# Adding 1e-9 to the row sums with a tensor-tensor operation, and converting the early weights one stage at a time

## The chip, the core and the metric

The kernel runs on one core of a Trainium2 chip. Five engines work side by side, each through its own queue in order: PE (TensorE, the matrix engine), DVE (VectorE), ACT (ScalarE), POOL (GpSimd) and SP (SyncE, which here issues the DMAs). They wait for each other by semaphores. The metric is the device time of one execution in microseconds (us).

## What is computed

Attention with a decay, and two feed-forward layers behind it, in 32-bit numbers:

```python
# attention: B, H, S, D = 4, 8, 576, 64
scores = matmul(q, k^T) / sqrt(D) + cum[:, None] - cum[None, :]   # cum = cumsum(log(clip(f)))
attn = exp(causal(scores) - rowmax)
attn = attn / (sum(attn) + 1e-9)
x = matmul(attn, v)                       # 2304 tokens x 512
# first layer: d_ff = 2048
x = softplus(x @ w_in) @ w_out
# second layer: d_ff = 1536
out = (sigmoid(x @ w_gate) * (x @ w_val)) @ w2_out
```

The weights arrive as 64-bit floating point numbers and are converted on the chip. Every 32-bit operand of a matmul is split into a high part in the matmul's own type and a low remainder, so that a product is three matmuls.

## The kernel before

**Attention.** The heads are taken two at a time: 16 pairs (p = 0 to 15). Of one pair, PE makes the score tiles (`scores`, L209 and L220, tile s), DVE adds the mask and finds the row extremes (`minimum`, L227, out to P and m), ACT takes exponentials and row sums (`exp`, L232), PE transposes P (`transposes`, L250, tile t, seven groups 0 to 6 that share two buffers), ACT takes the high part out of t (`evac_h`, L268, into PTah or PTbh), DVE the low part (`evac_l`, L272, into PTal or PTbl), which also frees the buffer of t, and PE multiplies with V (`pv`, L322, tile x). `rinv` (L275 to L280) adds 1e-9 to the nine columns of row sums of a pair (L278, a tile of 128x9) and takes the reciprocal (L279); PE transposes it (L284, tile rt, which takes one of the two t buffers), ACT copies it out (L289), and it goes through DRAM to be spread over rows. POOL splits q, k and v for coming pairs (L160 for the high parts Xh, Yh and V; L168 for the low parts Xl, Yl and V) and multiplies a finished pair with the reciprocal (L340, xs).

**The order of the work.** It is written out by hand: `WHEN` gives each step of a pair a time in units, a pair begins every `PERIOD` = 9 units, and the steps of all pairs, with a list `others` of (time, function), are sorted by time and issued in that order. `START` and `END` replace `WHEN` for the first and the last pair. So a number in these tables sets where an instruction stands in its engine's queue, and nothing else.

**Early weights.** Six blocks of the first layer's weights (wi0, wo0, wi1, wo1, wi2, wo2, each 128x512) are converted during the attention. `Weights` keeps seven stages for a block: LOAD (L463, a DMA of 512 KB issued by SP into one of four raw buffers), SCALE (ACT, L471), SHIFT, LOW, SIGN (DVE, L485, L487, L489: bit operations on 128x512 words that put the 64-bit number together; SHIFT has one input tile, LOW and SIGN have two, raw and w, all in SBUF), HI (ACT, L476) and LO (POOL, L479). `op(s)` does one stage for the next block that waits for it, and does nothing if none does; `tick` goes through all stages once. `TICKS` holds eight times of such ticks, and `LATE_TICKS` those behind the attention. Since SHIFT, LOW and SIGN are issued one behind the other in a tick, DVE does all three for one block in a row. I call that a burst; the eight ticks make six bursts.

**Behind the attention** come the two layers, where PE has matmuls to do nearly all the time.

Of the kernel before, what the change touches and what calls it, by code (L numbers as in the profile page):

```python
# [9 lines left out]
F32 = mybir.dt.float32  # L10
# [3 lines left out]
ALU = mybir.AluOpType  # L14
# [7 lines left out]
class Attention:  # L22
# [13 lines left out]
    def pools(self, pool, io_pool):  # L36
        self.vp = pool("at_v", 2)
        self.pp = pool("at_p", 2)
        self.sm = pool("at_small", 3)
        self.xp = pool("at_x", 2)  # L40
        self.io = io_pool("at_io", 2)
# [40 lines left out]
    def constants(self):  # L82

        nc, c, S = self.nc, self.c, self.S
        self.qrs = [c.tile([128, 640], F32, name=f"qr{i}") for i in range(2)]
        for q in self.qrs:
            nc.gpsimd.memset(q[0:64, 576:640], 0.0)
            nc.gpsimd.memset(q[64:128, 512:576], 0.0)
        self.nbs = [c.tile([128, S], F32R, name=f"nb{i}") for i in range(2)]
        nc.gpsimd.memset(self.nbs[0][64:128].bitcast(F32), 0.0)  # L90

        self.one = c.tile([128, 256], F32R, name="one")
        o = self.one[:].bitcast(F32)
        nc.gpsimd.memset(o, 0.0)
        for r, t in ((0, 128), (64, 192)):
            nc.gpsimd.memset(o[r:r + 2, 0:128], 1.0)
            nc.gpsimd.memset(o[r:r + 2, t:t + 64], 1.0)

        self.mask = c.tile([128, 512], F32, name="mask")
        nc.gpsimd.memset(self.mask, 0.0)  # L100
        nc.gpsimd.affine_select(self.mask, self.mask, pattern=[[-1, 512]], compare_op=ALU.is_ge,
                                fill=-8e9, base=384, channel_multiplier=1)
        self.mask4 = c.tile([128, S], F32, name="mask4")

    def constants2(self):
        nc, c, S = self.nc, self.c, self.S
        nc.gpsimd.memset(self.mask4, 0.0)
        for i in range(2):
            M = self.mask4[64 * i:64 * i + 64]
            nc.gpsimd.affine_select(M, M, pattern=[[-1, S]], compare_op=ALU.is_ge, fill=-8e9, base=512,  # L110
                                    channel_multiplier=1)
        nc.gpsimd.memset(self.nbs[1][:].bitcast(F32), 0.0)
        ident = c.tile([128, 128], F32, name="ident")
        nc.gpsimd.memset(ident, 0.0)
        nc.gpsimd.affine_select(ident, ident, pattern=[[-1, 128]], compare_op=ALU.not_equal,
                                fill=1.0, base=0, channel_multiplier=1)
        self.ident = ident

        self.vr = [c.tile([128, 5, 128], F32, name=f"vr{i}") for i in range(self.NVR)]
        for t in self.vr:  # L120
            nc.gpsimd.memset(t[64:128, 4], 0.0)
        self.pta = [[c.tile([128, 1152], F32R, name=f"PTa{w}{i}") for w in "hl"] for i in range(2)]
        self.ptb = [c.tile([128, 2368], F32R, name=f"PTb{w}") for w in "hl"]
        for t in self.ptb:
            for o, n in ((768, 128), (1792, 128), (2304, 64)):
                nc.gpsimd.memset(t[:, o:o + n].bitcast(F32), 0.0)
# [148 lines left out]
    def rinv(self, R, p):  # L275
        nc = self.nc
        r = self.sm.tile([128, 9], F32, tag="r", name=f"r{p}")
        nc.vector.tensor_scalar(r, R["sum"], 1e-9, None, op0=ALU.add)  # L278
        nc.vector.reciprocal(r, r)  # L279
        R["r"] = r  # L280

# [423 lines left out]
class Moe2:  # L705
# [53 lines left out]
    STEPS = 10  # L759
# [176 lines left out]

TICKS = [-79.5479, -7.81, 1.0296, 20.4876, 29.246, 38.239, 47.3352, 87.6118]
LATE_TICKS = [-7.39, 35.9211, 42.3787, 45.7979, 60.2136, 64.0078, 68.4722, 70.489, 70.7365, 71.6392, 73.755, 76.4625, 83.1312, 92.4907, 95.2063, 99.2562, 116.366, 144.939, 153.168, 159.446, 198.508]  # L940
X_STEPS = [-50.0345, -24.888, -24.7421, -11.1038, -4.6076, -2.1888, 2.7229, 20.2706]
UNITS = [58.5061, 83.1125]
# [3 lines left out]
def kernel(ctx: ExitStack, tc, q, k, v, f, w_in, w_out, w_gate, w_val, w2_out, out):  # L946
    nc = tc.nc
# [17 lines left out]
    W = Weights(nc, stage, 4)  # L965
# [10 lines left out]
    with ExitStack() as actx:  # L976
        ioctx = ExitStack()
        right = pools(actx, side="right")
        at = Attention(nc, q, k, v, f, xT, right, ps, dr)
        at.pools(right, pools(ioctx, side="right"))  # L980
        at.begin()
        end = at.PERIOD * at.NP
        m1 = []

        def open_pools():
            ioctx.close()
            chain = pool("chain", 1, **later)
            wb = pool("wb", 1, **later)
            W.add_slots(wb, tags("b", 2 * MORE))
            W.limit = EARLY + MORE  # L990
            m1.extend([chain, Moe1(nc, FC1, x1, yT, W, chain, ps)])

        others = [(t, W.tick) for t in TICKS] + [(end + t, W.tick) for t in LATE_TICKS]
        others += [(end + t, lambda k=k: x1.step(0, k)) for k, t in enumerate(X_STEPS)]
        others += [(end - .5, open_pools)]
        others += [(end + t, lambda u=u: m1[1].unit(u, 0)) for u, t in enumerate(UNITS)]
        at.run(others)
# [131 lines left out]
```

## Time and profile before

| | before |
|---|---|
| median of 3 runs | 1063.03 us (1062.92 to 1065.11) |
| profiled execution, its time and its span | 1063.44 us, span 1061.7 us |
| PE busy | 1027.5 us (97%) |
| DVE busy | 678.9 us (64%) |
| ACT busy | 455.2 us (43%) |
| POOL busy | 155.4 us (15%), all in the first 240 us |

The page's picture in 40 slices of 26.5 us shows PE at 4, 9, 9 and 8 tenths in the first four and at 9 (90% or more) from then on, DVE at 9 in slices 2 to 7, and POOL busy in the first nine slices alone. So the attention takes about the first 230 us, and what PE lacks is mostly in the first 100. An average over the whole span tells nothing here; the rows below are of stretches of the attention. A stretch is named by its start, and most are cut at the L278 of one pair and that of the next.

### The profile page before, as it was taken

The page shows a single profiled execution, that of the slowest core. Times are in us where ns is not written, and L with a number is a line of the kernel's source. Part 1 is how long each engine was busy: PE and PEld are TensorE (multiplying, and loading weights), DVE is VectorE, ACT ScalarE, POOL GpSimd, SP SyncE. Part 2 cuts the span into 40 slices and gives each one's busy share as a digit, 9 for nine tenths or more (in the row PEclk, how much of TensorE's full clock was granted, in tenths as well). Part 3 has the DMA queues.
Part 4 walks back from the last instruction along what each step waited for, and adds up shares of the span by engine and source line. Part 5 has one row for each costly group of instructions (what it writes and reads, how often), then busy time and mean ns, then how long its engine had stood idle before and what let it go on. Part 6 is the DMA issues. An engine that isn't in the chain of part 4 may idle for free.

```text
span 1061.7 us, 17894 instructions
## 1 busy us (share of the span) xinstructions
PE 1027.5 (97%) x6376; PEld 924.9 (87%) x6376; DVE 678.9 (64%) x1453; ACT 455.2 (43%) x989; POOL 155.4 (15%) x158
## 2 busy tenths in 40 slices
PE   4989999989999999999999999999999999999998
PEld 3767888878889999999999998999999999899997
DVE  5899999978955755745755556655655656555421
ACT  4678888866644434344343442222222222221121
POOL 7656777440000000000000000000000000000000
PEclk9999999999999999999999999999999999999999
DMA  6354454445534565564563599997887886686481
GB/s 167 94 151 128 130 145 125 130 138 183 188 128 172 197 233 178 192 236 170 193 225 126 201 358 362 341 314 248 279 262 231 288 261 230 228 296 215 141 274 63
DMA packets 129492, 218.23 MB, mean 206 GB/s; under 512 B 16174, under 2 KB 46526, under 8 KB 129404
## 3 DMA queue, kind: packets, MB, share of 16 engines
q1 hardware_dynamic: 126364, 212.08, 61.0%
q10 hardware_dynamic: 3040, 5.01, 1.4%
q8 instruction: 50, 0.82, 0.3%
q14 instruction: 38, 0.31, 0.1%
HBM read 171.21 MB, written 45.83 MB: 204 GB/s over the span
## 4 chain that ended last, share of the span: by engine, by line
PE 88%; DVE 7%; ACT 2%; issue 1%; DMA 1%; POOL 0%; ACTq 0%; SPq 0%; DVEq 0%; POOLq 0%
PE h L540 7%; PE h L541 7%; PE h L539 7%; PE s L220 5%; PE h_S L541 4%; PE h_S L539 4%; PE h_S L540 4%; PE x L322 4%; PE t L250 4%; PE h_A L539 3%; PE h_A L541 3%; PE h_A L540 3%; PE zX L900 3%; PE zX L901 2%; PE zX L902 2%; PE oY L540 2%
## 5 line engine op out<-in xcount | busy, mean ns | idle before, releaser
L541 PE MATMUL h<-xh,wi_l 128*128 128x448 f32 (+1 forms) x320 | 118.4, 370 | 0.0
L540 PE MATMUL h<-xl,wi_h 128*128 128x448 f32 (+1 forms) x320 | 118.4, 370 | 0.0
L539 PE MATMUL h<-xh,wi_h 128*128 128x448 f32 (+1 forms) x320 | 118.4, 370 | 0.0
L581 DVE TENSOR_TENSOR gl<-L,gh 128x448 fp32r<-128x448 f32 (+1 forms) x80 | 50.9, 637 | 99.4 <-ACT gh L580 88.5
L876 ACT CAST gh<-bl 128x512 fp32r<-128x512 f32 (+1 forms) x60 | 34.6, 579 | 168.6 <-DVE bl L847 141.5
L569 ACT ACTIVATE L<-h 128x448 f32<-128x448 f32 (+1 forms) x80 | 44.2, 552 | 142.3 <-PE h L541 131.1
L232 ACT ACTIVATE P<-P,m 128x128 f32<-128x128 f32 (+3 forms) x144 | 83.4, 583 | 13.1 <-DVE m L227 13.1
L540 PE MATMUL h_S<-x,ring 128*128 128x256 f32 x288 | 81.5, 283 | 0.0
L227 DVE CUSTOM_DVE_ANT_0 P<-s,mask 128x256 f32<-128x256 f32 (+3 forms) x144 | 70.7, 517 | 15.5 <-PE s L220 10.5
L539 PE MATMUL h_S<-x,ring 128*128 128x256 f32 x264 | 74.7, 283 | 0.0
L541 PE MATMUL h_S<-x,ring 128*128 128x256 f32 x264 | 74.7, 283 | 0.0
L250 PE MATMUL t<-ident,P 128*128 128x128 f32 x400 | 62.6, 293 | 7.0 <-DVE PTbl L272 4.0
L541 PEld LDWEIGHTS h<-xh,wi_l 128*128 128x128 f32 x320 | 60.1, 188 | 6.3
L539 PEld LDWEIGHTS h<-xh,wi_h 128*128 128x128 f32 x320 | 60.1, 188 | 6.3
L540 PEld LDWEIGHTS h<-xl,wi_h 128*128 128x128 f32 x320 | 60.1, 188 | 6.3
L250 PEld LDWEIGHTS t<-ident,P 128*128 128x128 f32 x400 | 47.0, 148 | 19.7 <-DVE PTbl L272 5.7
L845 ACT ACTIVATE bh<-bh 128x1024 f32<-128x1024 f32 x24 | 25.4, 1060 | 89.4 <-DVE bh L843 89.4
L681 DVE TENSOR_TENSOR l<-fw,sh 128x512 fp32r<-128x512 f32 x60 | 40.7, 686 | 35.8 <-ACT sh L680 35.7
L540 PEld LDWEIGHTS h_S<-x,ring 128*128 128x128 f32 x288 | 55.3, 192 | 0.0
L833 DVE TENSOR_TENSOR L<-h_S,L 128x256 f32<-128x256 f32 x48 | 20.3, 423 | 53.3 <-PE h_S L541 49.9
L540 PE MATMUL h_A<-x,ring 128*128 128x256 f32 x192 | 54.3, 283 | 0.0
L877 DVE TENSOR_TENSOR gl<-bl,gh 128x512 fp32r<-128x512 f32 (+1 forms) x60 | 38.0, 635 | 24.9 <-ACT gh L876 24.9
(233 smaller groups left out, 3079.5 us busy)
## 6 DMA issues: line engine op xcount, KB each, us to landing
ring<-sd_g SPq DMA_DIRECT2D x192, 256.0 KB
ring<-sd_v SPq DMA_DIRECT2D x192, 256.0 KB
raw_wi<-in_moe_w_in_dram SPq DMA_DIRECT2D x16, 512.0 KB
raw_wo<-in_moe_w_out_dram SPq DMA_DIRECT2D x16, 512.0 KB
fraw<-in_moe_w_gate_dram SPq DMA_DIRECT2D x12, 512.0 KB
fraw<-in_moe_w_out_dram SPq DMA_DIRECT2D x12, 512.0 KB
sd_g<-sh SPq DMA_DIRECT2D x24, 256.0 KB
sd_g<-l SPq DMA_DIRECT2D x24, 256.0 KB
```

The source lines that it names most:

```text
L220: nc.tensor.matmul(ps[h][:, 0:N], L[o], r[o, 0:N], start=j == 0, stop=j == n - 1)
L227: self.nc.vector.tensor_tensor_reduce(P, src, mask, -0.125, 3e38, op0=ALU.add, op1=ALU.min, accum_out=R["m"][:, t:t + 1])
L232: self.nc.scalar.activation(P, P, AF.Exp, bias=R["m"][:, t:t + 1], scale=-1.0, accum_out=R["sum"][:, t:t + 1])
L250: nc.tensor.transpose(ps[:, 128 * n:128 * n + 128], R["P"][:, o:o + 128], self.ident)
L322: nc.tensor.matmul(R["acc%d" % h][:, o:o + n], v, t[:, col:col + n], start=j == 0 and w == 0, stop=j == 1 and w == 1)
L539: nc.tensor.matmul(ps, ah, bh, start=start and i == 0, stop=False)
L540: nc.tensor.matmul(ps, ah, bl, start=False, stop=False)
L541: nc.tensor.matmul(ps, al, bh, start=False, stop=stop and i == n - 1)
L569: nc.scalar.activation(g, ph, AF.Softplus)
L581: nc.vector.tensor_sub(gl, s, gh)
L681: nc.vector.tensor_sub(l, w[n], h)
L877: nc.vector.tensor_sub(l, s, h)
```

## The change

Two parts. `rinv` adds the 1e-9 with `tensor_add` from a tile `eps` of 128x9 that POOL fills once in `constants`, in place of `tensor_scalar` with the number in the instruction; the instruction's other input and its output are as before. And `TICKS` gives way to `STEPS`, 44 pairs of (time, stage), each of which does one stage of one block: 8 LOAD, 6 each of SCALE, SHIFT, LOW, SIGN, HI and LO, the same work as the eight ticks.

```diff
+        self.eps = c.tile([128, 9], F32, name="eps")
+        nc.gpsimd.memset(self.eps, 1e-9)
...
-        nc.vector.tensor_scalar(r, R["sum"], 1e-9, None, op0=ALU.add)
+        nc.vector.tensor_add(r, R["sum"], self.eps)
...
-TICKS = [-79.5479, -7.81, 1.0296, 20.4876, 29.246, 38.239, 47.3352, 87.6118]
+STEPS = [(-7.81, 0), (1.294, 1), (3.294, 2), (12.294, 3), (14.294, 0), (21.294, 4), (22.794, 5), (24.294, 6),
...
-        others = [(t, W.tick) for t in TICKS] + [(end + t, W.tick) for t in LATE_TICKS]
+        others = [(t, lambda k=k: W.op(k)) for t, k in STEPS] + [(end + t, W.tick) for t in LATE_TICKS]
```

The DVE stages of `STEPS` fall at 9n + 3.294 units, one in each pair's period n = 0 to 14, and three more (LOW, in the periods 9, 11 and 13) at 9n + 6.381. PE's queue is the same before and after. On DVE, the first place is the period of pair 2 (names: r the reciprocal, t_0 and t_1 the transposes of groups 0 and 1, w_wi a block of weights). Before:

```order
L278 TENSOR_SCALAR r_505<-sum_327 128x9
L279 RECIPROCAL r_505<-r_505 128x9
L272 TENSOR_TENSOR PTal_168<-t_0_468,PTah_167 128x512
L272 TENSOR_TENSOR PTal_168<-t_1_478,PTah_167 128x512
L485 TENSOR_SCALAR w_wi_532<-w_wi_532 128x512
L487 SCALAR_TENSOR_TENSOR w_wi_532<-raw_wi_316,w_wi_532 128x512
L489 SCALAR_TENSOR_TENSOR w_wi_532<-raw_wi_316,w_wi_532 128x512
L227 ISA P_437,m_438<-s_1_0_519,mask 128x256
```

After, the burst is gone from there (line numbers are 2 higher), and what stands behind the next two `minimum` steps is one SIGN:

```order
L229 ISA P_427,m_428<-s_1_1_510,mask 128x256
L229 ISA m_428 128x1
L491 SCALAR_TENSOR_TENSOR w_wi_302<-raw_wi_257,w_wi_302 128x512
L274 TENSOR_TENSOR PTbl<-t_2_529,PTbh 128x512
L274 TENSOR_TENSOR PTbl<-t_3_537,PTbh 128x2x256
L229 ISA P_427,m_428<-s_0_0_550,mask 128x128
```

So three DVE instructions left the place ahead of the pair's score tile 1, and one stands ahead of the low parts of groups 2 and 3.

The second place is on DVE in the period of pair 9, later in the pair, ahead of the low part of group 4. Before:

```order
L272 TENSOR_TENSOR PTbl<-t_5_1965,PTbh 128x2x256
L227 ISA P_1806,m_1807<-s_2_0_1977,mask 128x384
L227 ISA m_1807 128x1
L272 TENSOR_TENSOR PTbl<-t_4_1972,PTbh 128x384
L227 ISA P_1997,m_1998<-s_4_2000,mask_122 128x576
```

After, with a LOW:

```order
L274 TENSOR_TENSOR PTbl<-t_5_1941,PTbh 128x2x256
L229 ISA P_1777,m_1778<-s_2_0_1955,mask 128x384
L229 ISA m_1778 128x1
L489 SCALAR_TENSOR_TENSOR w_wo_1866<-raw_wo_1561,w_wo_1866 128x512
L274 TENSOR_TENSOR PTbl<-t_4_1948,PTbh 128x384
L229 ISA P_1975,m_1976<-s_4_1978,mask_122 128x576
```

The same LOW stands in the periods 11 and 13. On POOL, LO still stands between the low part of V and the high part of q; on ACT, SCALE still stands behind the high parts of groups 0 and 1, and HI moves from there to behind the copy of rt.

## Rows read from the trace of the kernel before

**Rows 1.** Busy time by stretch, cut at L278; x is the count.

```profile
core 0: us, PE busy (x) PEld busy (x) DVE busy (x) ACT busy (x) POOL busy (x), PEclk, DMA share, GB/s
20.00:35.37 15.37, 10.87 (x64) 8.87 (x64) 14.79 (x30) 7.39 (x17) 10.45 (x8) 1.00 0.49 135
40.32:55.47 15.15, 13.41 (x96) 11.28 (x95) 13.71 (x34) 11.44 (x33) 9.70 (x9) 0.89 0.46 115
55.47:69.27 13.80, 12.09 (x96) 10.01 (x96) 13.38 (x36) 11.31 (x32) 8.70 (x9) 1.00 0.51 137
69.27:85.28 16.01, 13.61 (x96) 11.19 (x96) 14.04 (x34) 11.49 (x32) 9.73 (x9) 0.89 0.49 135
85.28:99.38 14.10, 12.11 (x96) 10.04 (x96) 13.68 (x36) 11.29 (x32) 8.99 (x9) 1.00 0.55 145
122.62:134.22 11.60, 11.60 (x96) 9.78 (x96) 10.69 (x33) 10.09 (x30) 7.93 (x8) 1.00 0.47 131
```

**Rows 2.** The same view, inside the first of these pairs.

```profile
46.65:50.06 3.41, 3.41 (x18) 2.83 (x19) 3.02 (x8) 1.76 (x5) 0.03 (x1) 0.50 0.02 3
```

**Rows 3.** Chain that ended last, by line, from 99.38 to 169.02 us.

```profile
by line: PE x L322 33.2%; PE s L220 29.0%; PE t L250 27.2%; PE s L209 9.1%; PE rt L284 1.8%
```

**Rows 4.** Instructions on tile w_wi: ns min/median/max, first and last start.

```profile
L485 DVE TENSOR_SCALAR w_wi<-w_wi x16: 414/422/1498, 21.0 to 300.0; 128x512 uint32<-128x512 uint32 x16
L487 DVE SCALAR_TENSOR_TENSOR w_wi<-raw_wi,w_wi x16: 681/686/1907, 22.5 to 300.7; 128x512 uint32<-128x512 uint32 x16
```

**Rows 5.** Timeline of a burst: start, length, engine; idle time before in brackets.

```profile
57.07 1.29 DVE L485 TENSOR_SCALAR w_wo<-w_wo 128x512 uint32<-128x512 uint32 x1
...
58.03 1.46 POOL L479 TENSOR_TENSOR wi_l<-w_wi,wi_h 128x512 fp32r<-128x512 f32 x1
...
58.39 1.65 DVE L487 SCALAR_TENSOR_TENSOR w_wo<-raw_wo,w_wo 128x512 uint32<-128x512 uint32 x1
...
61.16 0.38 PE L220 MATMUL s<-Yh,Xh 64*128 64x256 f32 x1 [1.45 <-DVE m L227]
```

**Rows 6.** Timeline of DVE in a pair without a burst.

```profile
122.62 0.95 DVE L278 TENSOR_SCALAR r<-sum 128x9 f32<-128x9 f32 x1
...
126.10 1.29 DVE L272 TENSOR_TENSOR PTbl<-t,PTbh 128x512 fp32r<-128x512 f32 x2 [0.43 <-ACT PTbh L268]
...
131.17 0.56 DVE L272 TENSOR_TENSOR PTbl<-t,PTbh 128x384 fp32r<-128x384 f32 x1
...
132.76 0.28 DVE L272 TENSOR_TENSOR PTbl<-t,PTbh 128x128 fp32r<-128x128 f32 x1
```

**Rows 7.** Timeline of POOL in the same pair.

```profile
122.11 1.44 POOL L340 TENSOR_TENSOR xs<-xs,rb 128x576 f32<-128x576 f32 x1
...
124.32 1.56 POOL L168 TENSOR_TENSOR V<-vr,V 128x640 fp32r<-128x640 f32 x1
129.47 0.73 POOL L160 TENSOR_SCALAR Xh<-qr 128x640 fp32r<-128x640 f32 x1 [3.58 <-PE s L220]
...
130.80 1.59 POOL L168 TENSOR_TENSOR Xl<-qr,Xh 128x640 fp32r<-128x640 f32 x1
```

**Rows 8.** Timeline of PE and ACT in the same pair.

```profile
127.59 0.84 PE L250 MATMUL t<-ident,P 128*128 128x128 f32 x5
...
127.79 0.26 ACT L289 COPY rt_sb<-rt 9x128 f32<-9x128 f32 x1 [0.24 <-PE rt L284]
...
132.90 1.09 PE L250 MATMUL t<-ident,P 128*128 128x128 f32 x8
```

**Rows 9.** Timeline of the start, pair 0.

```profile
22.31 0.59 ACT L268 CAST PTbh<-t 128x512 fp32r<-128x512 f32 x1 [0.29 <-PE t L250]
...
25.08 0.68 DVE L272 TENSOR_TENSOR PTbl<-t,PTbh 128x512 fp32r<-128x512 f32 x1
...
25.82 1.12 PE L250 MATMUL t<-ident,P 128*128 128x128 f32 x4 [2.69 <-DVE PTbl L272]
```

**Rows 10.** Timeline of POOL in the setup, behind its last memset.

```profile
6.08 1.88 POOL L168 TENSOR_TENSOR Yl<-kr,Yh 128x576 fp32r<-128x576 f32 x1 [1.25 <-DMA qr<-in_q_dram]
```

5 rows, old and new, of the table STEPS are left out of this document.

## The prediction, made before the changed kernel ran

> **What bounds the kernel now.** I read the stretches from one L278 to the next first, since every pair has the same 96 matmuls. A pair without a burst takes 11.60 us, with PE busy throughout; each of the four pairs that hold a burst takes 13.80 to 16.01 us, and PE lacks 1.7 to 2.4 us in it [rows 1]. Then the chain that ended last: through the pairs without a burst it is PE alone [rows 3]. So 11.60 us is PE's own length of a pair, DVE is idle for 11.60 - 10.69 = 0.91 us of it, and the excess of four pairs is what can be won. In two of them part of the time has a granted clock of half speed, the lower of TensorE's two levels (1.2 of 2.4 GHz): one such piece is 3.41 us long [rows 2], the other pair shows the same mean of 0.89 [rows 1].
>
> Why a burst costs so much is seen on DVE and POOL side by side. SHIFT lasts 422 ns in the median and up to 1498, LOW 686 and up to 1907 [rows 4]. In the burst at 57 us LOW starts at 58.39 while POOL works on LO from 58.03 to 59.49, and ends at 60.04, 0.55 behind POOL's end [rows 5]: it did no work before POOL was through. SHIFT behaves alike, with about 0.3 for its own work. L278 too: of 0.95 us, nearly all is waiting for POOL's L340, which ends at 123.55 [rows 6, 7]. So three DVE instructions of 1.8 us become 3.7 us, and PE waits for the `minimum` behind them, 1.45 us at 61.16 [rows 5].
>
> **Part 1, the bursts of four pairs leave.** 15.15 + 13.80 + 16.01 + 14.10 = 59.06 us, less 4 x 11.60 = 46.40, gives 12.66 us, the half-clock pieces included, since I take them to come from PE's gaps. Nothing else distinguishes these pairs: POOL's LO is in them, but a pair with LO alone would wait for nothing on PE. Gain **12.7**.
>
> **Part 2, the two bursts of the start leave.** Between 20 and 35.37 us PE lacks 15.37 - 10.87 = 4.5 us [rows 1], the most that can be won. One gap is of the burst's making: PE waits 2.69 us until the low part of a transpose has left its buffer [rows 9]. ACT has its high part ready at 22.90, DVE comes to the low part only at 25.08. Without the burst it starts at about 22.93, ends at 23.6, and PE goes on at 23.66 instead of 25.82: 2.16 us earlier. The second burst of the start lies beside the score matmuls that follow, so I give nothing for it. A SHIFT and a LOW now stand in this stretch; SHIFT falls into a wait for a transpose, LOW costs what it costs below, 0.25. Gain **1.9**, between 0.5 and 4.
>
> **Part 3, what the single steps cost.** Fifteen stand in the slot ahead of the low parts of groups 2 and 3. DVE is idle there for 0.43 us until 126.10 [rows 6], so it is free from 125.67. POOL works on V's low part until 125.88 [rows 7]. A LOW or SIGN that comes at 125.67 waits 0.2, works for 0.55 and lets the low parts start at 126.43 instead of 126.10, 0.33 late. They end at 127.39; the transposes of groups 5 and 4 need the buffer and start at 127.59 together with rt [rows 8]: a slack of about 0.1 in PE's queue. So 0.25 us of PE's time for each such step, and since PE is the bound, nothing gives it back. That is six pairs (2, 4, 5, 7, 8, 14): 1.5.
>
> SHIFT's own work is shorter, but it comes in the pair behind the one that has SIGN, HI and LO. HI follows ACT's copy of rt, which ends at 128.05 [rows 8]; at the 0.6 us of a cast of that size [rows 9] it ends at 128.65, and LO, 1.46 [rows 5], at 130.1, where POOL would have begun with Xh at 129.47 [rows 7]. POOL has no gap from there to V's low part, so all of it comes some 0.6 us late, 0.7 with what DVE's own turn adds, and SHIFT waits until 126.6 and ends at 126.9: the low parts start 0.8 late, PE loses 0.7. Five pairs (3, 6, 9, 11, 13): 3.5. Were POOL on time, it would be 0.1 each, the lower bound.
>
> The three LOW of the second slot (pairs 9, 11, 13) come between a `minimum` and the low part of group 4 at 131.17 [rows 6]. There POOL works on Xl from 130.80 to 132.39 [rows 7]. LOW waits until then, works 0.55, and the low part of group 4 starts 1.7 us late, that of group 6, now at 132.76 to 133.04, about 1.55 late. The eight transposes at 132.90 [rows 8] need these buffers, the second four at about 133.3 the one of group 6: slack 0.25, so PE loses 1.3 each, 3.9 in all. In pairs 10 and 12, behind them, PE and DVE have fallen behind POOL, which is then done with V: SIGN costs some 0.1 each, 0.2.
>
> Sum of part 3: 1.5 + 3.5 + 3.9 + 0.2 = **9.1** lost. Its bounds: 3.5, when SHIFT meets no lag and DVE's idle 0.91 takes up most of the rest; 15, when most steps wait for a whole POOL instruction.
>
> **Part 4, 1e-9 from a tile.** The memset of `eps` falls ahead of the 1.25 us that POOL waits for the first heads' data [rows 10]: nothing. The new L278 reads two tiles in SBUF. The nearest row is LOW, which also reads two and waits for POOL [rows 5]; so I let it wait as before, change 0. Its wait costs PE nothing in a pair such as that at 122.62, where DVE comes back to its place before PE needs it [rows 1, 3].
>
> No row shows a plain tensor-tensor operation with both inputs in SBUF beside POOL's work. The Trainium skill (SBUF — State Buffer, Who interferes with whom) states that such an instruction contends with a GpSimd instruction that reads SBUF; by that rule the change of L278 gives nothing, and the sum is the same.
>
> HI, SCALE, LO and the loads: ACT has 1.5 us idle in a pair [rows 1], and HI or SCALE takes 0.6 of it. Each LOAD is one DMA on SP's queue; six of the eight come later than before, so the start has two fewer to share the DMA engines with, and the later ones pass q, k and v loads that a pair does not need for most of its length. I count nothing. If a load of v landed late, POOL's work on V would slip and with it the slot of part 3.
>
> **The sum.** Against the profiled execution's 1063.44 us (span 1061.7, and 1.7 around it; the median is 0.4 lower): 1063.44 - 12.66 - 1.9 + 9.1 = 1057.98. I say **1058.0**. Behind the attention everything is PE's, so what the attention gains stays.
>
> **The rivals.**
> - Steps nearly free. For it: DVE has 0.91 us idle per pair, and L278's wait shrinks by as much as DVE comes late. Against it: the wait of PE is local, for two buffers of t. Then part 3 costs 3.7 and the start gives 2.5, both towards their better bounds: 1063.44 - 12.66 - 2.5 + 3.7 = 1052.
> - Most of it given back: part 3 costs 13 to 15, since POOL lags in more pairs than those behind LO. 1063.44 - 14.56 + 14 = 1062.9, no change.
> - Slower. Each of the 17 steps behind the start waits for a whole POOL instruction, as LOW does at 58.39: it then takes 1.65 in place of 0.69 [rows 4, 5], less the 0.43 idle and the 0.1 slack, so PE loses 1.1, 17 x 1.1 = 18.7; at the same time gaps of that length bring the half clock back once, 1.7 us for a piece of 3.41 [rows 2]. 1063.44 - 14.56 + 20.4 = 1069.3. It decides from the point at which a step costs 14.56/17 = 0.86 us on average. For it: the waits of SHIFT and LOW in the bursts [rows 4, 5]. Against it: those bursts were issued beside V's low part and LO, the new first slot where POOL is just coming free.
> - L278 no longer waits. Where POOL makes it wait longest, DVE would be back earlier, and the lag behind LO would matter less: at most 1 to 2 us, 1056.5; inside the forecast's range.
>
> **How the numbers follow.** Forecast (1055 to 1060.8, L278's rival in it): 0.52. Steps nearly free: 0.20. Given back: 0.16. Slower: 0.12. A measurement of this kernel tells about 0.2% from no change, 2.1 us; faster means below 1060.9, which the first two hold: 0.72; same 0.16; slower 0.12. The range: 1051 leaves out a little of the nearly-free case, 1064 most of the slower one and some of the given-back one, together 2 in 10.
>
> **What the profile after would show.** Part 1: the stretches of pairs 2 to 5 between 11.6 and 12.4 us, no half clock in them. Part 2: PE's gap of 2.69 near 25 us down to about 0.5, the L278 of pair 1 near 38.4 in place of 40.32. Part 3: LOW and SIGN of the first slot near 0.8 us, SHIFT near 1.2 in the pairs behind LO, the three LOW of the second slot near 1.8 with PE waiting for the low parts of groups 4 and 6, pairs 9, 11 and 13 the longest, some 13.5 us. Part 4: the new L278 still near 0.95. The prediction falls if pairs 9, 11 and 13 stay at 11.6, if a half-clock piece appears in them, or if L278 drops to 0.17.

## The result and the profile after

The changed kernel takes 1052.77 us in the median of 5 runs (1051.47 to 1058.02), the kernel before beside it 1063.44 (1062.92 to 1065.20): a ratio of 0.9892, with a 95% interval from 0.9866 to 0.9919. It is faster by about 10.7 us, twice the forecast 5.4, and inside the range. One of the ten executions of a kernel below, e_burst_old, took 2553.21 us, and its ratio is of the other nine.

Every pair has one `rt` on PE (the transpose of `rinv`, L284 before, L286 after), so its start is a mark that can be compared between kernels. The last pair's stands at 219.73 us before and at 208.98 after: the attention alone gives 10.75. The profiled execution gives half of that back in the first layer (its time is 1058.02, and that this equals the forecast of 1058.0 is chance); the last section shows that single executions differ there, with the change and without it. So I compare kernels by these marks, and by times only beside them. The `rinv` and the rt of a pair fall into the period of the pair behind it: what I call pair 9 below is the period of pair 9, and it begins with the L280 of pair 8 at 119.43 us.

**Pairs 2 to 5.** The view of busy time by stretch, cut at L280 as [rows 1] at L278 (columns as there); the last row is pair 9.

```profile
37.22:49.53 12.31, 12.11 (x98) 10.06 (x96) 11.06 (x32) 10.79 (x32) 8.94 (x9) 1.00 0.35 99
49.53:61.03 11.50, 11.50 (x95) 9.68 (x94) 11.06 (x32) 10.56 (x31) 7.90 (x8) 1.00 0.41 120
61.03:72.67 11.64, 11.64 (x96) 9.86 (x96) 11.34 (x32) 10.12 (x30) 7.95 (x8) 1.00 0.67 184
72.67:84.31 11.64, 11.64 (x96) 9.86 (x96) 11.34 (x32) 10.51 (x31) 8.77 (x9) 1.00 0.46 131
...
119.43:132.65 13.22, 12.30 (x98) 10.01 (x98) 13.08 (x35) 11.03 (x31) 9.75 (x9) 1.00 0.55 155
```

The four stretches that took 59.06 us take 47.09, with PE busy throughout in three of them, and the granted clock is 1.00 where two of [rows 1] had 0.89. Pair 9 is now the long one: PE lacks 0.92 us in it.

**The start.** Timeline of PE (start, length; idle before in brackets), which answers to [rows 9]:

```profile
23.73 1.12 PE L252 MATMUL t<-ident,P 128*128 128x128 f32 x4 [0.55 <-DVE PTbl L274]
```

The gap of 2.69 us is 0.55. The score matmuls behind it are shorter too; the same one of them before and after:

```profile
28.55 0.44 PE L209 MATMUL s<-Yh,Xh 128*128 128x288 f32 x1
25.97 0.30 PE L211 MATMUL s<-Yh,Xh 128*128 128x288 f32 x1
```

**The first place of a single step.** Timeline of DVE with a SIGN (L491) in pair 8 and a SHIFT (L487) in pair 9, behind LO:

```profile
107.79 0.94 DVE L280 TENSOR_TENSOR r<-sum,eps 128x9 f32<-128x9 f32 x1
...
110.78 0.82 DVE L491 SCALAR_TENSOR_TENSOR w_wi<-raw_wi,w_wi 128x512 uint32<-128x512 uint32 x1
111.52 1.27 DVE L274 TENSOR_TENSOR PTbl<-t,PTbh 128x512 fp32r<-128x512 f32 x2
...
119.43 1.38 DVE L280 TENSOR_TENSOR r<-sum,eps 128x9 f32<-128x9 f32 x1
...
122.80 0.60 DVE L487 TENSOR_SCALAR w_wo<-w_wo 128x512 uint32<-128x512 uint32 x1
123.32 1.28 DVE L274 TENSOR_TENSOR PTbl<-t,PTbh 128x512 fp32r<-128x512 f32 x2
```

and of POOL there:

```profile
109.48 1.57 POOL L170 TENSOR_TENSOR V<-vr,V 128x640 fp32r<-128x640 f32 x1
113.84 1.28 POOL L481 TENSOR_TENSOR wi_l<-w_wi,wi_h 128x512 fp32r<-128x512 f32 x1 [2.79 <-ACT wi_h L478]
115.10 0.72 POOL L162 TENSOR_SCALAR Xh<-qr 128x640 fp32r<-128x640 f32 x1
...
121.56 1.55 POOL L170 TENSOR_TENSOR V<-vr,V 128x640 fp32r<-128x640 f32 x1
```

SIGN waits for POOL's V (until 111.05) and ends 0.55 behind it; SHIFT waits for the V of its pair (until 123.11) and ends 0.29 behind it.

**The second place.** LOW (L489) in pair 9, with POOL, DVE and PE in turn:

```profile
127.84 1.58 POOL L170 TENSOR_TENSOR Xl<-qr,Xh 128x640 fp32r<-128x640 f32 x1
...
128.20 1.77 DVE L489 SCALAR_TENSOR_TENSOR w_wo<-raw_wo,w_wo 128x512 uint32<-128x512 uint32 x1
129.89 0.55 DVE L274 TENSOR_TENSOR PTbl<-t,PTbh 128x384 fp32r<-128x384 f32 x1
...
131.23 0.28 DVE L274 TENSOR_TENSOR PTbl<-t,PTbh 128x128 fp32r<-128x128 f32 x1
...
130.58 0.63 PE L252 MATMUL t<-ident,P 128*128 128x128 f32 x4 [0.56 <-DVE PTbl L274]
131.56 0.66 PE L252 MATMUL t<-ident,P 128*128 128x128 f32 x4 [0.35 <-DVE PTbl L274]
```

LOW starts 0.36 into POOL's `Xl`, ends 0.55 behind it, and PE waits twice, 0.56 and 0.35 us, for the low parts of groups 4 and 6 that DVE makes at 129.89 and 131.23. The chain that ended last, by line from 84.31 to 157 us, was PE alone in [rows 3]; now these LOW are on it, and some of DVE's work behind them:

```profile
by line: PE x L324 28.9%; PE t L252 25.3%; PE s L222 24.8%; PE s L211 5.8%; DVE PTbl L274 3.5%; DVE P L229 3.2%; DVE w_wo L489 2.3%; DVE w_wi L489 2.3%; PE rt L286 1.7%; issue 1.4%; DVE PTal L274 0.6%; DVE m L229 0.3%
```

**The 1e-9.** Instructions on tile eps (ns min/median/max, first and last start):

```profile
L280 DVE TENSOR_TENSOR r<-sum,eps x16: 166/942/1401, 32.5 to 207.5; 128x9 f32<-128x9 f32 x16
L105 POOL MEMSET eps<- x1: 113/113/113, 4.2 to 4.2; 128x9 f32 x1
```

L278 before had 171, 950 and 1350 ns: the new form waits as the old one.

### The profile page after: what moved, and what is told of

Its sections match the earlier page's. It is cut to its first block, busy times and chain, and to the rows that moved or that the text cites. A ratio compares the mean times of both kernels' runs of the same rounds, so it can differ in the third digit from the quotient of the medians.

```text
span 1056.2 us, 17893 instructions
## 1 busy us (share of the span) xinstructions
PE 1029.0 (97%) x6376; PEld 921.5 (87%) x6376; DVE 673.4 (64%) x1453; ACT 454.6 (43%) x989; POOL 154.9 (15%) x159
## 4 chain that ended last, share of the span: by engine, by line
PE 88%; DVE 6%; ACT 2%; DMA 2%; issue 1%; SPq 0%; POOL 0%; ACTq 0%; DVEq 0%; POOLq 0%
PE h L541 7%; PE h L542 7%; PE h L543 7%; PE s L222 5%; PE x L324 4%; PE t L252 4%; PE h_S L543 4%; PE h_S L541 4%; PE h_S L542 4%; PE h_A L541 3%; PE h_A L543 3%; PE h_A L542 3%; PE zX L902 3%; PE zX L903 3%; PE zX L904 2%; PE oY L541 2%
```

## The experiments

The marks of all kernels, in us from the start of the span. "rt 8 to 9" is the stretch from the rt of pair 8 to that of pair 9 and holds the LOW of the second place in pair 9; "rt 10 to 11" holds that of pair 11.

| kernel | first rt | rt 8 to 9 | rt 10 to 11 | last rt | first to last | ratio of times to before (95%) |
|---|---|---|---|---|---|---|
| before | 38.99 | 11.60 | 11.60 | 219.73 | 180.74 | 1 |
| after | 35.89 | 12.81 | 12.80 | 208.98 | 173.09 | 0.9892 (0.9866 to 0.9919) |
| after_again | 34.78 | 12.81 | 12.81 | 207.46 | 172.68 | 0.9902 (0.9884 to 0.9920) |
| e_eps | 38.93 | 11.61 | 11.61 | 219.73 | 180.80 | 1.0005 (0.9987 to 1.0023) |
| e_steps | 36.31 | 12.80 | 12.80 | 209.68 | 173.37 | 0.9896 (0.9867 to 0.9925) |
| e_start | 38.92 | 12.80 | 12.81 | 211.62 | 172.70 | 0.9923 (0.9893 to 0.9952) |
| e_slot | 36.02 | 11.83 | 11.82 | 207.38 | 171.36 | 0.9885 (0.9857 to 0.9914) |
| e_burst_old | 38.44 | 13.14 | 13.16 | 219.82 | 181.38 | 0.9985 (0.9963 to 1.0006) |
| e_burst_idle | 35.76 | 11.63 | 11.61 | 210.63 | 174.87 | 0.9917 (0.9886 to 0.9948) |
| e_double | 36.16 | 13.00 | 12.99 | 211.60 | 175.44 | 0.9912 (0.9884 to 0.9940) |
| e_noeps | 35.83 | 12.97 | 12.94 | 208.56 | 172.73 | 0.9902 (0.9874 to 0.9929) |
| e_best | 35.01 | 11.84 | 11.84 | 206.18 | 171.17 | 0.9884 (0.9863 to 0.9906) |
| e_best2 | 38.47 | 11.83 | 11.84 | 208.66 | 170.19 | 0.9882 (0.9854 to 0.9910) |
| e_best3 | 34.57 | 11.84 | 11.81 | 204.62 | 170.05 | 0.9837 (0.9815 to 0.9860) |

The kernel once more shows what repeats.

> The changed kernel once more, to see which parts of its trace repeat. All theories: last pair's rt within 0.5 us of 208.98. In its first profiled execution PE's matmuls on tile h took 206.7 ns from start to start from about 410 us on, in most other traces 202.7; if that belongs to single executions and not to the kernel, this trace may show either, and the times fall into two groups some 5 us apart for before and after alike.

From the first to the last rt the two traces differ by 0.41 us, and in the pairs 9 and 11 by 0.01 at most. The first rt moves by 1.1: the start has some play of its own. The last rt, 1.52 earlier, missed the 0.5 that was expected.

### Which part of the change does it

Before with the new form alone:

```diff
+        self.eps = c.tile([128, 9], F32, name="eps")
+        nc.gpsimd.memset(self.eps, 1e-9)
...
-        nc.vector.tensor_scalar(r, R["sum"], 1e-9, None, op0=ALU.add)
+        nc.vector.tensor_add(r, R["sum"], self.eps)
```

> The kernel before with the first part of the change alone: the 1e-9 comes from the tile eps by a tensor-tensor operation, the eight ticks stay. My theory (the new form waits for POOL as the old one did): no change, 1063 us within 1, the instruction still near 0.95 us in the median and up to 1.4. Rival (the new form no longer waits, and a part of the gain of 10.7 us comes from it): it takes about 0.17 us in every pair, and the time falls by 1 to 3 us.

```profile
L280 DVE TENSOR_TENSOR r<-sum,eps x16: 167/952/1246, 35.3 to 218.2; 128x9 f32<-128x9 f32 x16
```

The last rt stands where it stood before, and the instruction waits as it did. (The median, 1067.07, lies above the expected 1063, and so does that of before beside it, 1065.39; the two belong together, and the ratio is 1.0005.) After with the old form:

```diff
-        nc.vector.tensor_add(r, R["sum"], self.eps)
+        nc.vector.tensor_scalar(r, R["sum"], 1e-9, None, op0=ALU.add)
```

> The changed kernel with the tensor-scalar form put back, so the second part alone. My theory: the whole gain is in the steps, 1052.8 us within 1. Rival (the form of the 1e-9 has a share): 1054 to 1056 us.

The length from first to last rt is that of after within 0.3 us, and the ratio the same. The form has no share; the whole gain is in the steps. (The median here, 1055.65, falls among the rival's 1054 to 1056; but that of before beside it is 1065.39, 2 us over the 1063.44 of the first comparison, and the ratio decides. The medians of e_slot, 1054.63, and e_start, 1058.91, taken beside the same runs of before, lie 4.3 and 3.4 us above the times expected of them; 2 us of that are in before too, the rest is not explained.)

### Does L280's wait matter at all

```diff
-        nc.vector.tensor_add(r, R["sum"], self.eps)
-        nc.vector.reciprocal(r, r)
+        nc.vector.reciprocal(r, R["sum"])
```

> The changed kernel without the 1e-9 (left out: the reciprocal is taken straight from the sums), so DVE has neither that instruction nor its wait. Theory A (the wait lies in time that DVE has to spare, or the next instruction takes it over): the last pair's rt stays within 0.3 us of 208.98. Theory B (where LO makes POOL late, the wait of 1.38 us is what costs these pairs 0.2 us each): the end comes 1 to 2 us earlier.

DVE in the pair whose L280 took 1.38 us:

```profile
119.23 0.21 DVE L280 RECIPROCAL r<-sum 128x9 f32<-128x9 f32 x1
119.35 1.23 DVE L274 TENSOR_TENSOR PTal<-t,PTah 128x512 fp32r<-128x512 f32 x2
```

Nothing waits in its place: the reciprocal, which reads one tile of 128x9, lasts 0.20 to 0.21 us in all 16 pairs, with POOL at work beside it in 15. And still the attention is shorter by 0.36 us only (or longer by 0.05, against after_again); the last rt stands 0.42 earlier, where theory A had 0.3 at most and B 1 to 2. The stretches with a SHIFT behind LO do fall from 11.84 to 11.64, so theory B's 0.2 is real, but the stretches behind them take it back (12.97 and 12.94 in place of 12.81 and 12.80).

### The second place

The entries of `STEPS` for these three LOW:

```diff
-(87.381, 3)
+(85.85, 3)
...
-(105.381, 3)
+(104.1, 3)
...
-(123.381, 3)
+(121.85, 3)
```

> The changed kernel with the three LOW of the second place (pairs 9, 11, 13) moved earlier on DVE, to where POOL has nothing to do in the changed kernel's trace: in pairs 9 and 13 ahead of both L339, in pair 11 between them. Theory A (their price is waiting for POOL's instruction): each takes 0.69 us instead of 1.77, 1.75 and 0.96, pairs 9 and 11 fall from 12.8 us to 11.6 to 11.9, the time by 2 to 2.8 us, to about 1050.3. Theory B (DVE has simply one instruction too many in these pairs, since it has some 0.9 us idle in a pair and SHIFT stands in them already): LOW takes 0.69, but the pairs stay at 12.3 us or more, and the time falls by less than 1.2 us.

```profile
125.14 0.69 DVE L489 SCALAR_TENSOR_TENSOR w_wo<-raw_wo,w_wo 128x512 uint32<-128x512 uint32 x1
```

Theory A: LOW takes 0.69 and 0.67 us in pairs 9 and 11, their stretches fall by 1.0 each to 11.8 with the same work on DVE, so the amount of that work is not what cost the 1.0. The place ahead of both L339 and the one between them are worth the same. From the first to the last rt it is 1.7 us less than in after, a little under the 2 to 2.8 expected, since the pair of the last SIGN became 0.25 longer (a stretch in which single executions differ as well: 12.03 in after_again, 12.40 in e_steps); in the times, whose intervals are 6 us wide, that can't be seen by itself.

### The start

```diff
-STEPS = [(-7.81, 0), (1.294, 1), (3.294, 2), (12.294, 3), (14.294, 0), (21.294, 4), (22.794, 5), (24.294, 6),
-         (28.294, 1), (30.294, 2), (39.294, 3), (41.294, 0), (48.294, 4), (49.794, 5), (51.294, 6), (55.294, 1),
+TICKS = [-79.5479, -7.81, 1.0296]
+STEPS = [(22.794, 5), (24.294, 6), (55.294, 1),
```

> The changed kernel with the two bursts of the start put back (the first three ticks of the kernel before), and single steps for the four blocks that are left. In the traces so far the start gained 3.1 us where the prediction had 1.9, and the granted clock rose to full 4.2 us earlier in the changed kernel (25.38 in place of 29.58 us). Theory A (the burst holds PE up in the start, and the later rise of the clock comes from that gap): the 1e-9's instruction of pair 1 is back near 40.3 us, the clock rises near 29.6, and the time is 3.1 us longer less some 0.4 for the six single steps that pairs 1 to 5 lose, about 1055.5. Theory B (the start's gain is chance of the one execution, or of the order of loads): the pair 1 mark stays near 37.5 us and the time at 1052.8.

Theory A, in DVE's and PE's timelines:

```profile
24.40 0.69 DVE L491 SCALAR_TENSOR_TENSOR w_wi<-raw_wi,w_wi 128x512 uint32<-128x512 uint32 x1
25.01 0.68 DVE L274 TENSOR_TENSOR PTbl<-t,PTbh 128x512 fp32r<-128x512 f32 x1
...
25.74 1.97 PE L252 MATMUL t<-ident,P 128*128 128x128 f32 x8 [2.46 <-DVE PTbl L274]
27.36 0.59 PE L211 MATMUL s<-Yh,Xh 128*128 128x288 f32 x1
27.75 0.44 PE L211 MATMUL s<-Yh,Xl 128*128 128x288 f32 x1
...
28.98 0.30 PE L211 MATMUL s<-nb,one 128*128 128x288 f32 x1
```

The first rt is back at 38.92, 3.03 later than in after; the steps that its first pairs lack give 0.39 from there to the last rt, so the end is 2.64 later. Both as expected. The first rt stands at 38.92 to 38.99 in all three traces with these bursts, and at 34.57 to 36.31 in nine of the eleven without; the other two are explained below.

### What a burst costs

The three DVE steps of four middle blocks in one row again (9n + 2.3 units, n = 5, 8, 10 and 12, where the bursts of before stood), HI and LO single and later; and the same rows at 9n + 4.85. Block 1 as the example:

```diff
-(30.294, 2), (39.294, 3), ... (48.294, 4), (49.794, 5), (51.294, 6)
+(47.3, 2), (47.301, 3), (47.302, 4), (51.5, 5), (53.95, 6)
```

```diff
-(30.294, 2), (39.294, 3), ... (48.294, 4), (49.794, 5), (51.294, 6)
+(49.85, 2), (49.851, 3), (49.852, 4), (51.5, 5), (53.95, 6)
```

> The changed kernel with SHIFT, LOW and SIGN of the four middle blocks issued in one row again, in the pairs 5, 8, 10 and 12 at the place in the pair where the bursts of before stood (ahead of score tile 1, POOL at work on V); HI and LO stay single, LO at the end of the pair. Theory A (a burst costs what it waits for POOL): the three take 3 us or more instead of 1.8, PE waits 1.5 to 2 us for the score tile, the four pairs take 13.3 to 14 us; against the single steps that leave (3.4 us in all in the changed kernel's trace) the last pair's rt comes 4 to 5 us later than its 208.98, about 1057 us. Theory B (a burst costs its three instructions, wherever they stand; LO beside it was what made it long): they take 1.8 us, the pairs 12.2 to 12.5, the end of the attention moves by less than 1.

> The same kernel with the four bursts later in the pair, ahead of both L339, where POOL had nothing to do in the changed kernel's trace for some 1.4 us more. Theory A (waiting for POOL): the three take 1.8 to 2.3 us, the four pairs 12 to 12.5 us (DVE has about 0.9 us idle and 0.8 in the wait of the 1e-9's instruction), and the last pair's rt comes 5 to 7 us earlier than with the bursts at the old place. Theory B (the three instructions cost the same wherever they stand): the two kernels end within 1 us of each other.

The old place, POOL, DVE and PE:

```profile
76.96 1.55 POOL L170 TENSOR_TENSOR V<-vr,V 128x640 fp32r<-128x640 f32 x1
...
77.52 1.28 DVE L487 TENSOR_SCALAR w_wo<-w_wo 128x512 uint32<-128x512 uint32 x1
78.83 0.69 DVE L489 SCALAR_TENSOR_TENSOR w_wo<-raw_wo,w_wo 128x512 uint32<-128x512 uint32 x1
79.55 0.69 DVE L491 SCALAR_TENSOR_TENSOR w_wo<-raw_wo,w_wo 128x512 uint32<-128x512 uint32 x1
...
80.64 0.73 PE L222 MATMUL s<-Yh,Xh 64*128 64x256 f32 x2 [1.13 <-DVE m L229]
```

The idle place, DVE and PE:

```profile
77.94 0.42 DVE L487 TENSOR_SCALAR w_wo<-w_wo 128x512 uint32<-128x512 uint32 x1
78.39 0.69 DVE L489 SCALAR_TENSOR_TENSOR w_wo<-raw_wo,w_wo 128x512 uint32<-128x512 uint32 x1
79.12 0.69 DVE L491 SCALAR_TENSOR_TENSOR w_wo<-raw_wo,w_wo 128x512 uint32<-128x512 uint32 x1
...
80.62 0.51 PE L324 MATMUL x<-PTah,V 128*128 128x256 f32 x2 [1.15 <-DVE xs L339]
```

Neither theory comes out whole. At the old place SHIFT waits for POOL's V and the row lasts 2.72 us; at the idle place it lasts 1.87 and waits for nothing. Yet the pairs with a burst take 13.14 to 13.16 at the one and 13.01 to 13.24 at the other: three instructions in a row cost 1.4 to 1.6 us at either, because at the idle place PE waits for L339 behind them instead. So the waiting for POOL, on which theory A put the price, makes only 0.1 between these two places. (They can differ in slack as well; what the wait costs at one and the same place was not measured.) In before the bursts without half clock cost 2.2 and 2.5 [rows 1]; the 0.7 to 1.0 more goes with LO, which there ran beside LOW [rows 5]. That share is a difference between kernels; I did not isolate it.

The last rt of the old place comes 10.84 us later than in after, where A had 4 to 5; 2.55 of that lie in the start, ahead of the bursts. From the first to the last rt the two kernels differ by 6.5 us, as A said, but not for A's reason. The bursts' own stretches make 0.3 of it. The clock makes 3.6: in two of four pairs at the old place a piece of half clock begins 1.29 and 2.04 us after the end of PE's gap of 1.1 us (the first of these gaps, and both stretches, columns as in [rows 1]),

```profile
117.39 0.72 PE L222 MATMUL s<-Yh,Xh 64*128 64x256 f32 x2 [1.10 <-DVE m L229]
...
118.68:122.09 3.41, 3.16 (x15) 2.50 (x15) 2.04 (x7) 2.65 (x9) 0.05 (x1) 0.50 0.21 62
145.98:149.40 3.42, 3.42 (x17) 2.65 (x16) 2.23 (x5) 3.13 (x10) 1.24 (x2) 0.50 0.59 170
```

and the stretches with these pieces take 13.41 and 13.49 us without a burst in them. The other two pairs at the old place, with gaps of 1.13 us, and the four gaps of 1.14 to 1.15 at the idle place brought no such piece. The rest, 2.5, lies mostly in the last pairs; its cause stays open.

### How much slack the first place has

```diff
             v.scalar_tensor_tensor(u, hi, 0x80000000, u, op0=ALU.bitwise_and, op1=ALU.bitwise_or)
+            if self.limit == 6:
+                v.scalar_tensor_tensor(u, hi, 0x80000000, u, op0=ALU.bitwise_and, op1=ALU.bitwise_or)
```

> The changed kernel with each of the six early SIGN issued twice (the second gives the same words again), so 0.69 us more for DVE in the first place of the pairs 2, 5, 8, 10, 12 and 14. It sizes the slack behind that place, which the prediction put at 0.1 us and which looks larger, since single steps cost almost nothing there. Theory A (the transposes of group 4 wait for the copy of rt anyway, so there are some 0.3 us to spare, once): each of the six pairs 0.3 to 0.5 us longer, 2 to 3 us in all, about 1055. Theory B (DVE's idle time and the wait of the 1e-9's instruction take up even this): under 0.5 us in all. Theory C (the prediction's slack of 0.1 is right and the single steps are cheap for another reason): 0.6 each, 3.6 us.

The stretches with a doubled SIGN take 11.93 in place of 11.64, and the ones behind them 12.05 in place of 11.84: 0.5 us for 0.69 more on DVE, 2.35 in all. Theory A: a further 0.2 us finds room, and the rest is PE's loss.

### Better places

HI one pair later, so that LO follows V's low part; SHIFT and all LOW but the first at 9n + 4.85. The first of these entries (each block's are moved alike, and the loads 4 to 9 units earlier):

```diff
-(22.794, 5), (24.294, 6), (28.294, 1), (30.294, 2), (39.294, 3)
+(19.294, 1), (22.85, 2), (28.294, 5), (29.3, 6), (40.85, 3)
```

> The changed kernel with the steps laid where no POOL work is met: SIGN stays in the first place; HI of a block goes to the next pair, so LO stands right behind V's low part, where POOL is idle afterwards, and no longer pushes V back; SHIFT and all LOW but the first go ahead of both L339, one to a pair. Theory A (the 0.2 us of the pairs with HI and LO and of those behind them come from LO making POOL late, the 1.2 us of pairs 9 and 11 from LOW waiting for POOL): pairs 5 to 12 all take 11.6 to 11.7 us, the last pair's rt comes 2.5 to 3.2 us earlier than in the changed kernel, the time near 1050. Theory B (a part of it is DVE's load, whatever POOL does): the pairs with SIGN and SHIFT stay at 11.8 or more, and the end comes under 2 us earlier.

Stretches with SIGN, SHIFT, HI or LO take 11.61 to 11.66: the 0.2 of the pairs behind LO is gone, as A said. But each LOW ahead of both L339 costs 0.2 (11.81 to 11.84), with no POOL work beside it; that A had not seen. The last SIGN took 1.90: POOL went from V straight on to `Yl` for the last pair. In all 1.9 us less than after from the first to the last rt, under the 2 that divided A from B. (The last rt itself, of which the expectation spoke, stands 2.80 earlier, within A's range; but 0.88 of that is the earlier start.) Neither theory comes out whole.

Then two LOW and the last SIGN moved once more:

```diff
-(40.85, 3)
+(39.294, 3)
...
-(67.85, 3)
+(66.294, 3)
...
-(129.294, 4), (130.794, 5)
+(130.85, 4), (131.6, 5)
```

> The kernel just before with three steps laid anew: the LOW of the pairs 4 and 7 back in the first place, where POOL is through with V and no LO of the converter is near, and the last SIGN (it took 1.90 us there, and its pair 12.85) ahead of both L339, its HI and LO behind. My theory (in the first place a step costs 0.03 where POOL has just come free, ahead of both L339 about 0.2, and a step that meets POOL up to 1.2): the pairs with LOW of 4 and 7 fall from 11.81 and 11.84 us to 11.65, the last SIGN's from 12.85 to 12.2, the last pair's rt stands 1.0 us earlier than 206.18 less what the start differs. Rival (the last SIGN's pair is long because of the last pair's own order of work): 0.4 us earlier.

The two LOW back in the first place take their stretches from 11.81 and 11.84 to 11.65 and 11.66, the last SIGN's falls from 12.85 to 12.16: 0.98 us, as expected. But the start is late, as it was in e_burst_old, and DVE and POOL show where it begins: the first SHIFT.

```profile
24.30 1.60 POOL L170 TENSOR_TENSOR Xl<-qr,Xh 128x640 fp32r<-128x640 f32 x1
25.81 1.46 POOL L170 TENSOR_TENSOR Yl<-kr,Yh 128x576 fp32r<-128x576 f32 x1
...
24.57 2.98 DVE L487 TENSOR_SCALAR w_wi<-w_wi 128x512 uint32<-128x512 uint32 x1
```

In after it met `Xl` alone:

```profile
23.57 1.58 POOL L170 TENSOR_TENSOR Xl<-qr,Xh 128x640 fp32r<-128x640 f32 x1
...
24.44 0.99 DVE L487 TENSOR_SCALAR w_wi<-w_wi 128x512 uint32<-128x512 uint32 x1
```

The L280 of pair 0 comes 1.20 us later than in after, the first rt 2.58 later. The other 1.4 us fall into a piece of half clock between the two, which stands at the same place in e_burst_old (33.34 us) and in no other trace:

```profile
33.38:36.79 3.41, 3.41 (x16) 2.68 (x15) 2.14 (x11) 2.64 (x10) 1.40 (x3) 0.50 0.02 6
```

Between 30 and 33 us PE has gaps of 0.23 and 0.42 us there, and one of 0.42 in after; whether the wait of SHIFT brings the piece is not shown. The last edit moves SHIFT to where POOL is through:

```diff
-STEPS = [(-7.81, 0), (1.294, 1), (3.294, 2), (10.294, 0), (12.294, 3), (19.294, 1), (21.294, 4), (22.85, 2),
+STEPS = [(-7.81, 0), (1.294, 1), (10.294, 0), (11.5, 2), (12.294, 3), (19.294, 1), (21.294, 4), (22.85, 2),
```

> The kernel just before with the first SHIFT moved too. It stands beside POOL's two low parts for pair 1 (24 to 27 us): in eight traces without the bursts of the start it took 0.7 to 1.4 us and ended 0.3 behind one POOL instruction, in two it took 3.0 and ended 0.3 behind the second of them, and just these two traces have the first pair's rt at 38.4 to 38.5 us instead of 34.8 to 36.3. Now it stands behind the low part of group 6, when POOL is through. Theory A (the start's late traces come from this wait): SHIFT takes 0.42 us, the first rt stands at 34.8 to 36.3 us, the last at 205 to 206.5, and no execution is late for that reason: the median 1050 us or a little less, the highest not over 1054. Theory B (what is late in these two traces is the clock, half from 33.3 to 36.8 us, for a reason of its own): the first rt can come out at 38.4 here too, with SHIFT at 0.42.

```profile
28.31 0.42 DVE L487 TENSOR_SCALAR w_wi<-w_wi 128x512 uint32<-128x512 uint32 x1
```

SHIFT takes 0.42 us, the first rt stands at 34.57, the last at 204.62, and the five runs lie between 1047.85 and 1049.80 us: median 1048.66, with before at 1066.94 beside it, ratio 0.9837 (0.9815 to 0.9860). It beats both kernels: its last rt is 4.36 and 2.84 us ahead of the two traces of after, and its five times lie below the lowest of theirs, 1051.47 and 1052.78. The ratio makes it look a little better than it is, since seven of the nine executions of before beside it took 1065.53 us and more, over the 1063.44 of the first comparison. Theory A's numbers came out, the two marks even 0.2 and 0.4 us ahead of its ranges, though a single trace cannot exclude that the late start would have stayed away by chance.

## Why the prediction was right, and where it was not

The direction, the mechanism of the gain and each place named were right. The forecast time was 5.2 us too high, nearly all of it in part 3: the single steps were put at 9.1 us and cost 4.0. By its sum, what happened is the rival "steps nearly free" (1052), which had a chance of 0.20 against the forecast's 0.52. Term by term:

- **Part 1, 12.7 for the bursts of four pairs.** Measured 11.97 by the L278 and L280 marks. The missing 0.7 is mostly pair 2, at 12.31: from rt to rt its stretch takes 12.12 in e_start too, which has no step there, so this is no price of steps. No half clock came in these pairs, as forecast. But the reading of why a burst is dear held in part only. POOL's instructions do make SHIFT and LOW long; yet e_burst_idle shows that three in a row cost 1.4 us without any such wait. What the change gains, it gains because one instruction fits the slack of a pair and three do not; and in two pairs of before the half clock came on top, which e_burst_old and e_eps show to follow PE's gaps only sometimes.
- **Part 2, 1.9 for the start.** Measured 3.10 (L278 of pair 1 from 40.32 to 37.22). The gap gave 2.14 where 2.16 stood. What the sum lacked is a term for the clock: PE's eight matmuls for the 128x288 tiles take from 25.35 to 26.59 us after and took from 27.44 to 29.64 before, 0.96 less. One of them lasts 0.30 after and 0.44 before, and the trace's record of a granted clock of 1.00 begins at 25.38 in after and at 29.58 in before; e_start, with the bursts, has the 0.44 and, from 28.71 on, where that record begins, the 0.30. Over all traces the record begins at 28.72 to 30.17 in the three with these bursts and at 24.34 to 26.80 in the eleven without, so the later rise goes with the bursts; but the 0.96 is in part luck, since the eight take from 1.24 to 2.20 us in the kernels without the bursts. Only the gap is the same in every one of ten (0.55; e_best3, with SHIFT moved, has 0.96 there).
- **Part 3, 9.1 for single steps.** Measured 4.0, in the stretches from rt to rt against those without a step. *The first place, LOW and SIGN:* 0.03 to 0.09 each where 0.25 stood. The wait (0.82 us long, 0.8 forecast) was right; the low parts start 3.73 us behind L280 against 3.48 [rows 6], so 0.25 late, and PE lost 0.03: the slack is 0.2, not 0.1. *SHIFT behind LO:* 0.23 in three stretches and 0.44 in the last, where 0.7 stood; the first has none. LO took 1.28, not the 1.46 that it took beside a burst [rows 5]; POOL's Xh then began 7.31 us behind L280 instead of 6.85, a lag of 0.46 for which I had 0.6 to 0.7, and L280 itself waited 0.44 longer for it, so that SHIFT came later and waited only 0.2. The low parts start 0.41 late; less the slack of 0.2 that is about the 0.23. *The second place:* 1.2 each in pairs 9 and 11 where 1.3 stood, with LOW at 1.77 and 1.75 (1.8 forecast) and PE's two waits at the places named; in pair 13 LOW took 0.96 and the stretch 0.32, since POOL stood otherwise there. That LOW ends 0.55 behind POOL's instruction each time, and e_slot, where it meets none, give POOL as the cause. *What the sum leaves:* the three parts make 11.97 + 3.10 - 4.0 = 11.1 where 10.75 was measured; 0.39 lies behind the last step on DVE (rt 13 to 14, 11.62 against 11.23, but 11.30 in after_again).
- **Part 4, nothing for the 1e-9.** Right: e_eps, e_steps and e_noeps. The Trainium skill (SBUF — State Buffer, Who interferes with whom) says that a DVE instruction with two SBUF inputs contends with a GpSimd instruction that reads SBUF. The trace agrees: 942 ns in the median for 128x9 elements, 166 at the least, and 15 of the 16 end 0.01 to 0.03 us behind an instruction of POOL. The old form, with one SBUF input, did the same (950, 171, 15 of 16). With that the rival "L278 no longer waits" fell, and so did its price of 1 to 2 us: without the instruction, 0.36 at most.
- **The rivals "given back" and "slower".** They needed 14 us for part 3, or 0.86 us a step. Two of the 18 steps cost more than that (the LOW of pairs 9 and 11), the others 0.44 or less.
- **Behind the attention** "what the attention gains stays": right, but for the play of single executions below.

## What to carry to other kernels

On an engine that has a little slack in each period, spread its extra work one instruction to a period: what is lost is only what goes beyond the slack at that place, and a burst of three went beyond it at both places tried. Then look, for each instruction with a wait that no semaphore explains, which instruction of the other engine it ends behind, and put it where that engine has nothing to do for longer than the instruction lasts; check also who waits for what stands behind it. And to size such edits use a mark inside the program, here the rt of the last pair: most of what separates the kernels here is smaller than what single executions differ by.

## What the runs showed of the hardware

- **A SHIFT can wait through two instructions of POOL.** In the start it ended 0.3 us behind one POOL instruction in most traces, and in e_burst_old and e_best2 behind the second, after 3.08 and 2.98 us, though it had been issued 0.18 and 0.27 us into the first; in e_slot, issued 0.45 into it, and in before, issued 0.19 into it, it got in behind the first (1.43 and 1.50). Why it missed its turn is open.
- **The same PE gap does not always bring half clock**: gaps of 1.09 to 1.13 us in a pair did in two of four cases, gaps of 1.14 to 1.15 in none of four. Before and e_eps each have two such pieces in the pairs, but the second at 77.37 us, behind a gap of 2.14, in the one, and at 91.61 us in the other, where a gap of 2.06 at 75.31 brought none.
- **Nine columns can wait as long as a whole tile.** L278 and L280, in either form, last 0.16 to 0.17 us alone and up to 1.41 beside POOL; the reciprocal of the same 128x9 elements, in e_noeps, never over 0.21.
- **The first layer runs at one of two rates.** Stretches of PE in the same program, after and after_again (columns as in [rows 1]):

```profile
410.00:600.00 190.00, 190.00 (x921) 172.59 (x920) 111.07 (x203) 80.04 (x146) 0.00 (x0) 1.00 0.55 191
```

```profile
410.00:600.00 190.00, 190.00 (x938) 175.68 (x937) 111.38 (x205) 80.03 (x147) 0.00 (x0) 1.00 0.56 194
```

PE is busy throughout at a granted clock of 1.00 in both, and does 921 matmuls in the one and 938 in the other: 206.3 and 202.6 ns each. The slower rate set in at about 390 us in after, and is there in e_eps, e_burst_old and a part of e_steps too, with bursts and without. It costs some 5 us where it lasts to the layer's end; what sets it in I don't know.
